# Decayed linear attention and two feed-forward layers on one core: moving the token sums of two joint blocks from GpSimd to VectorE

## The chip, the cores and the metric

The kernel runs on one core of a Trainium2 chip. The metric is the device time of one execution in microseconds; of several executions the median is given. The trace is that of one profiled execution.

## The reference

`x` has 1536 tokens of 512 features, made by a blocked linear attention with a decay for each head; two feed-forward layers follow.

```python
x = attention(q, k, v, lam)                # (B*S, H*D) = (1536, 512)
h = x @ w_in;   g = h * tanh(softplus(h));      x = g @ w_out     # 512 -> 2048 -> 512, "mish"
h = x @ w_in2;  g = h * clip(h + 3, 0, 6) / 6;  out = g @ w_out2  # 512 -> 2048 -> 512, "hswish"
```

## The kernel before

The 1536 tokens are three blocks of 512 (`k` = 0, 1, 2). Every value that a matmul reads is a pair of fp32r numbers, a rounded high part and a low part, so a product is three matmuls. `split` makes such a pair: ScalarE writes the high part (L101), VectorE subtracts it from the source for the low part (L105).

The first layer is a loop of 48 steps (`STEPS`). Its last 16 steps finish blocks 0 and 1, whose results lie in `part[0]` and `part[1]`, each 128 x 4 x 512. The last product of block 1 is still outstanding when the loop ends: `emit_g2(STEPS - 2 + j, [f])` runs it inside the next stage, and `evacuate` (L418) adds its four pieces from PSUM to `part[1]` at the points (j, f) of `LEFT`: (1, 2), (1, 3), (2, 0), (2, 1).

The second layer is done by Strassen-like products of seven terms. The third block (k = 2) goes first, over eight weight pairs, j = 0 to 7 ("pairs" below). In each pair there are four fills, f = 0 to 3 (names a, b, c, d). A fill (L827) multiplies seven terms in all into PSUM bank 0 (in pairs 0 and 1 banks 0 and 1 in turn), ScalarE copies the bank out (L968), and VectorE adds the copies into four features (L971, L975, L978, L980). Then `gate` applies the activation (ScalarE L854, VectorE L855), `feature_sums` forms four differences on VectorE (L875, tile `FS`), and `feature_part` splits the features into the tiles `G` (in the trace `lowB` or `up`), one pair later. `second` (L846) multiplies `G` by the output weights, two pairs later (`LAG`), in four pieces between the fills (`GAPS`). So in pair j TensorE does the fills of pair j and the second products of pair j - 2, which need the second feature part of pair j - 2, made in pair j - 1. The products of `second` accumulate in PSUM banks that the outstanding product of block 1 occupied: term 6 needs the bank of the first `evacuate`, term 7 that of the second, 5 and 3 those of the others.

After the pairs, blocks 0 and 1 are multiplied jointly (`joint`, L1032), eight weight pairs again, on seven token terms `XJ[0]` to `XJ[6]`, read in the order 0, 2, 5, 4, 3, 6, 1. They are made from `part[0]` (halves B11, B21) and `part[1]` (B12, B22) by the generator `joint_sums`, which the pair loop advances at the points of `SUMS`. Four of the seven are differences; GpSimd forms them in place, on 128 x 1024 fp32 values each (L473).

Within this stage the instructions of TensorE, VectorE and ScalarE are held in program order on each engine (`hold`); those of GpSimd are not held, and run when their inputs are there. Weights come by DMA from the SyncE queue: `bring(j)` at the end of pair j fetches those of later pairs into slots (`SLOT`).

Of the kernel before, what the change touches and what calls it, by code (L numbers as in the profile page):

```python
# [16 lines left out]
ALU = mybir.AluOpType  # L17
# [5 lines left out]
def decay_attention__mish_ffn__hswish_ffn_kernel(  # L23
# [8 lines left out]
    nc = tc.nc  # L32
# [9 lines left out]
    def hold(engine, ins):  # L42
        if engine in held:
            tc.keep_in_program_order(ins)
        return ins
# [57 lines left out]
    def split_lo(lo, hi, src, scale=1.0):  # L103
        if scale == 1.0:
            hold("vector", nc.vector.tensor_tensor(out=lo, in0=src, in1=f32(hi), op=ALU.subtract))  # L105
        else:
            hold("vector", nc.vector.scalar_tensor_tensor(  # L107
                out=lo, in0=src, scalar=scale, in1=f32(hi), op0=ALU.mult, op1=ALU.subtract
            ))
# [233 lines left out]
    def split(hi, lo, src, scale=1.0, on_vector=False):  # L343
        if on_vector:
            hold("vector", nc.vector.tensor_scalar(out=hi, in0=src, scalar1=scale, scalar2=None, op0=ALU.mult))
        else:
            split_hi(hi, src, scale)
        split_lo(lo, hi, src, scale)
# [56 lines left out]
    def g_lo(n):  # L405
        split_lo(g_t[n][:, 1], g_t[n][:, 0], f_t.pop(n))
# [60 lines left out]

    def joint_sums(a, b):

        B11, B12, B21, B22 = a[:, 0:2], b[:, 0:2], a[:, 2:4], b[:, 2:4]  # L470

        def sub(o, x, y):
            nc.gpsimd.tensor_tensor(out=o, in0=x, in1=y, op=ALU.subtract)  # L473

        def put(i, src):
            split(XJ[i][:, 0], XJ[i][:, 1], src)

        put(0, B11)
        yield
        put(2, B21)  # L480
        yield
        sub(B11, B12, B11)
        sub(B12, B22, B12)
        put(1, B22)
        sub(B22, B22, B11)
        sub(B21, B21, B22)
        yield
        put(3, B11)
        yield
        put(4, B12)  # L490
        yield
        put(5, B22)
        yield
        put(6, B21)
        yield

    def words(flat, i):
# [77 lines left out]
    def operand(slot, i):  # L575
        at = 512 * i
        for ap in SLOT[slot]:
            if at < ap.shape[1]:
                return ap[:, at:at + 512].rearrange("p (a n) -> p a n", a=2)
            at -= ap.shape[1]  # L580
# [226 lines left out]
    def acc_of(j):  # L807
        return ACC if j < NPAIR else ACCS[(j - SECONDS) // NPAIR]

    def block_of(j):  # L810
        return NBLK - 1 if j < NPAIR else (j - SECONDS) // NPAIR

    def pair_of(j):
        if j < NPAIR:
            return down[j]
        j -= SECONDS
        return j if j < NPAIR else 2 * NPAIR - 1 - j
# [14 lines left out]
    def whole(*ms):  # L832
        return tuple((m, (0, 1)) for m in ms)

    def second(j, parts):
        at = j + LAG if j < NPAIR else j
        nth = j % NPAIR if j < NPAIR else (j - SECONDS) % NPAIR
        first, last = nth == 0, nth == NPAIR - 1
        slot = slot_at[at][pair_of(j), 1]
        for m, halves in parts:  # L840
            gi, wi = SECOND[m]
            g = G[j][0][:, gi] if gi < 3 else G[j][1][:, gi - 3]
            w, acc = operand(slot, wi), BANK[:, acc_of(j)[m]].rearrange("p (s n) -> p s n", s=2)
            for i in halves:
                for q, (a, b) in enumerate(PASS):
                    hold("tensor", nc.tensor.matmul(  # L846
                        acc[:, i], lhsT=g[:, a, i * 128:i * 128 + 128], rhs=w[:, b],
                        start=(first and i == 0 and q == 0), stop=(last and q == 2), skip_group_check=True,
                    ))
            if last and (j < LAST or m != 3):  # L850
                close(block_of(j), m, acc_of(j))
# [11 lines left out]
    def features(j):  # L863
        if j < NPAIR:
            return FH[j % 2]
        return FJ[pair_of(j)][:, 1024 * block_of(j):1024 * block_of(j) + 1024].rearrange("p (i n) -> p i n", i=4)
# [10 lines left out]
    def feature_part(j, i):  # L877
        g, src = G[j][i], (features(j)[:, 1:4], FS[j % 2])[i]
        split(g[:, :, 0], g[:, :, 1], src)
# [15 lines left out]
    def close(k, m, acc):  # L895
        def scaled(o, m):
            hold("scalar", nc.scalar.activation(out=o, in_=BANK[:, acc[m]], func=ACTF.Copy, scale=SIXTH))

        def added(o, m, b):
            hold("vector", nc.vector.scalar_tensor_tensor(  # L900
                out=o, in0=BANK[:, acc[m]], scalar=SIXTH, in1=b, op0=ALU.mult, op1=ALU.add
            ))

        if not seen:
            if k == NBLK - 1:
                tile_ = stage_p.tile([128, 4, 512], F32, tag="st2", name="rest")
                rest[:] = [tile_[:, i] for i in range(4)]
            else:
                rest[:] = [work[:, 2048:2560], work[:, 2560:3072], two[:, 0], two[:, 1]]
        p1, p7, c12, c21 = rest  # L910
        c11, c22 = p1, p7
        q = [x.rearrange("p (s n) -> p s n", s=2) for x in rest]
        seen.add(m)
        if m == 1:
            scaled(p1, 1)
        elif m == 7:
            added(p7, 7, c12)
        elif m == 4 and not {6, 7} <= seen:
            scaled(c21, 4)
        elif m == 6:  # L920
            added(c12, 6, p1)
        if m == 7 and 4 in seen:
            plus(c21, c21, p7)
            store(k, 1, 0, q[3])
        elif m == 4 and {6, 7} <= seen:
            added(c21, 4, p7)
            store(k, 1, 0, q[3])
        if m in (2, 6) and {2, 6} <= seen:
            added(c11, 2, p1)
            store(k, 0, 0, q[0])  # L930
        if m == 5:
            added(c12, 5, c12)
        if {4, 5, 6, 7} <= seen and m in (4, 5):
            added(c22, 5, p7)
            store(k, 1, 1, q[1])
        if m == 3:
            added(c12, 3, c12)
            store(k, 0, 1, q[2])
        if len(seen) == 7:
            seen.clear()  # L940
# [12 lines left out]

    GAPS = (whole(1) + ((6, (0,)),), ((6, (1,)),) + whole(7), whole(4, 2), whole(5, 3))
    LEFT = ((1, 2), (1, 3), (2, 0), (2, 1))
    SUMS = ((0, 1), (0, 3), (2, 3), (4, 1), (5, 1), (6, 1), (7, 1))
    made = joint_sums(part[0], part[1])
    held.update(("tensor", "vector", "scalar"))
    for j in range(NPAIR):
        F = FH[j % 2]  # L960
        if j == 0:
            g_lo(STEPS - 1)
        for f, (name, ms) in enumerate(FILLS):
            bank_ = BANK[:, f % 2 if j < LAG else 0]
            fill(j, ms, bank_)
            n = 256 * len(ms)
            c = COPY[name]
            hold("scalar", nc.scalar.activation(out=c, in_=bank_[:, 0:n], func=ACTF.Copy))  # L968
            c = c.rearrange("p (i n) -> p i n", n=256)
            if f == 1:  # L970
                hold("vector", nc.vector.tensor_tensor(  # L971
                    out=F[:, 2:4], in0=COPY["a"].unsqueeze(1).to_broadcast([128, 2, 256]), in1=c, op=ALU.add
                ))
            elif f == 2:
                hold("vector", nc.vector.tensor_tensor(  # L975
                    out=F[:, 0:4:3], in0=F[:, 3:4].to_broadcast([128, 2, 256]), in1=c, op=ALU.add
                ))
                hold("vector", nc.vector.tensor_tensor(out=F[:, 1], in0=F[:, 0], in1=c[:, 1], op=ALU.add))  # L978
            elif f == 3:
                hold("vector", nc.vector.tensor_tensor(out=F[:, 0:4:3], in0=F[:, 0:4:3], in1=c, op=ALU.add))  # L980
            if j < LAG:
                emit_g2(STEPS - 2 + j, [f])
            else:
                second(j - LAG, GAPS[f])
            if f == 0 and j in (1, 2):
                FS.append(g_p.tile([128, 4, 256], F32, tag="g", name=f"FS{j}"))
            if f == 0 and j > 0:
                gates(j - 1, 0, 3)
                feature_sums(j - 1)
            elif f == 3:  # L990
                gates(j, 1, 1)
            elif j > 0:
                feature_part(j - 1, f - 1)
            if (j, f) in LEFT:
                evacuate(STEPS - 1, [LEFT.index((j, f))])
            if (j, f) in SUMS:
                next(made)
        bring(j)
    assert next(made, None) is None
    gates(NPAIR - 1, 0, 3)  # L1000
    second(NPAIR - 2, whole(1, 4, 2))
    feature_sums(NPAIR - 1)
    for i in range(2):
        feature_part(NPAIR - 1, i)
    second(NPAIR - 2, whole(6, 7, 5, 3))
    bring(NPAIR)
    second(NPAIR - 1, whole(*CLOSING))
# [139 lines left out]
```

## Time and profile before

| | us |
|---|---|
| median of 3 runs | 556.02 (555.74 to 556.15) |
| the profiled execution | 555.68 |
| its span, first to last instruction | 553.4 |
| the third block's eight pairs in the span | 301 to 382 |
| the joint products | 392.6 to 468.8 |

The rows below are from the profiled execution, whose time lies 2.28 us above its span. Times of a row count from the span's start. In a timeline, a row is a start, a duration, the engine, the line, the operation, output<-inputs with their shapes, and a count; in brackets is how long the engine had been idle before it, and what ended the idle time. Rows of a count above one merge instructions that follow each other. Matmuls are pipelined, so the durations of neighbouring rows overlap. PE is TensorE, DVE VectorE, ACT ScalarE, POOL GpSimd.

### The profile page before, as it was taken

The numbers are of one execution on the slowest core, as the hardware profiler recorded it, in microseconds if no ns is written. First come the engines' busy times: TensorE is split into PE (matmuls) and PEld (weight loads), VectorE is DVE, ScalarE is ACT, GpSimd is POOL, SyncE is SP. The second block draws the span as 40 slices with busy tenths as digits, with TensorE's granted clock in tenths as the row PEclk, the third lists the DMA queues.
The fourth block names the chain that finished last, engine by engine and source line by source line (L and its number), as shares of the span: only waits on it lengthen the run. The fifth ranks groups of instructions, "written<-read, shape, count | busy, mean of one in ns | idle before, by whom it ended". The sixth has DMA issues, their size and how long they took to land.

```text
span 553.4 us, 8899 instructions
## 1 busy us (share of the span) xinstructions
PE 543.8 (98%) x3552; PEld 475.2 (86%) x3552; DVE 392.6 (71%) x590; ACT 288.8 (52%) x425; POOL 33.5 (6%) x28
## 2 busy tenths in 40 slices
PE   8999999999999999999999989999999999999997
PEld 4887888888888888888888979999888888999996
DVE  6668875561136767796772899988677889978853
ACT  2457898873255756867482644655132434433420
POOL 1761000000000000000000033000000000000000
PEclk9999999999999999999999998999999999999999
DMA  8995556450045998889979953978655467961832
GB/s 288 411 398 205 174 195 200 153 167 25 0 153 208 370 357 278 324 307 427 371 275 411 428 230 125 379 259 324 246 189 210 165 234 252 386 295 55 292 130 77
DMA packets 23625, 137.99 MB, mean 249 GB/s; under 512 B 2208, under 2 KB 5408, under 8 KB 17440
## 3 DMA queue, kind: packets, MB, share of 16 engines
q1 hardware_dynamic: 23584, 137.43, 66.0%
q8 instruction: 28, 0.46, 0.3%
q14 instruction: 13, 0.11, 0.1%
HBM read 104.91 MB, written 32.51 MB: 248 GB/s over the span
## 4 chain that ended last, share of the span: by engine, by line
PE 94%; DVE 3%; DMA 2%; issue 0%; SPq 0%; ACT 0%; DVEq 0%; ACTq 0%
PE bank L371 24%; PE bank L380 24%; PE bank L846 21%; PE bank L1032 14%; PE bank L827 7%; PE bank L194 2%; PE bank L242 2%; DMA raw<-att 2%; PE bank L248 1%; PE bank L234 1%; DVE FS L875 1%; DVE part L418 0%; DVE work L978 0%; SPq L152 0%; ACT X L101 0%
## 5 line engine op out<-in xcount | busy, mean ns | idle before, releaser
L105 DVE TENSOR_TENSOR g<-x,g 128x512 fp32r<-128x512 f32 x48 | 33.0, 690 | 55.3 <-ACT g L401 51.6
L380 PE MATMUL bank<-g,up 128*128 128x512 f32 x288 | 70.3, 389 | 0.0
L371 PE MATMUL bank<-X,up 128*128 128x512 f32 x288 | 69.2, 389 | 0.0
L400 ACT ACTIVATE x<-bank 128x512 f32<-128x512 f32 x48 | 28.5, 593 | 69.6 <-PE bank L371 69.6
L371 PEld LDWEIGHTS bank<-X,up 128*128 128x128 f32 x288 | 54.1, 188 | 11.2
L380 PEld LDWEIGHTS bank<-g,up 128*128 128x128 f32 x288 | 53.6, 188 | 10.6
L371 PE MATMUL bank<-X,lowA 128*128 128x512 f32 x180 | 43.2, 389 | 0.0
L380 PE MATMUL bank<-g,lowA 128*128 128x512 f32 x180 | 43.2, 389 | 0.0
L380 PEld LDWEIGHTS bank<-g,lowA 128*128 128x128 f32 x180 | 33.8, 188 | 7.0
L371 PEld LDWEIGHTS bank<-X,lowA 128*128 128x128 f32 x180 | 33.8, 188 | 7.0
L107 DVE SCALAR_TENSOR_TENSOR lowA<-spare,lowA 128x1792 fp32r<-128x1792 f32 x16 | 32.4, 2023 | 10.3 <-ACT lowA L101 10.3
L846 PE MATMUL bank<-up,up 128*128 128x256 f32 x270 | 36.5, 288 | 1.6 <-DVE up L105 1.6
L846 PEld LDWEIGHTS bank<-up,up 128*128 128x128 f32 x270 | 34.6, 197 | 1.8 <-DVE up L105 1.8
L101 ACT ACTIVATE lowA<-spare 128x1792 fp32r<-128x1792 f32 x16 | 27.3, 1704 | 6.7 <-DVE spare L602 6.1
L1032 PE MATMUL bank<-X,lowA 128*128 128x512 f32 x120 | 29.3, 389 | 0.0
L401 ACT ACTIVATE g<-bank 128x512 fp32r<-128x512 f32 x48 | 28.5, 594 | 0.0
L332 ACT ACTIVATE tops<-ring 128x512 f16<-128x512 bf16 (+1 forms) x32 | 25.3, 790 | 4.0 <-DMA ring<-w 3.8
L1032 PEld LDWEIGHTS bank<-X,lowA 128*128 128x128 f32 x120 | 22.5, 188 | 4.6
L380 PE MATMUL bank<-g,lowB 128*128 128x512 f32 x108 | 25.9, 389 | 0.0
L371 PE MATMUL bank<-X,lowB 128*128 128x512 f32 x108 | 25.7, 390 | 0.0
L332 ACT ACTIVATE ring<-tops 128x512 int32<-128x512 int16 (+1 forms) x32 | 25.1, 783 | 0.8
L337 DVE SCALAR_TENSOR_TENSOR ring<-ring 128x512 int32<-128x512 int32 x24 | 16.6, 691 | 11.9 <-ACT ring L332 11.9
(192 smaller groups left out, 1038.1 us busy)
## 6 DMA issues: line engine op xcount, KB each, us to landing
wc<-lowA SPq DMA_DIRECT2D x16, 1792.0 KB, 9.9
lowA<-wc SPq DMA_DIRECT2D x15, 1792.0 KB, 9.2
up<-wc SPq DMA_DIRECT2D x13, 1792.0 KB, 8.5
ring<-w SPq DMA_DIRECT2D x24, 511.8 KB, 3.6
raw<-att SPq DMA_DIRECT2D x16, 512.0 KB, 10.2
ring<-w SPq DMA_DIRECT2D x8, 1023.5 KB, 7.2
spare<-w SPq DMA_DIRECT2D x8, 1023.5 KB, 8.1
early<-att SPq DMA_DIRECT2D x8, 512.0 KB, 10.3
```

The lines of the kernel that those rows point to most:

```text
L101: hold("scalar", nc.scalar.activation(out=hi, in_=src, func=ACTF.Copy, scale=scale))
L105: hold("vector", nc.vector.tensor_tensor(out=lo, in0=src, in1=f32(hi), op=ALU.subtract))
L107: hold("vector", nc.vector.scalar_tensor_tensor(out=lo, in0=src, scalar=scale, in1=f32(hi), op0=ALU.mult, op1=ALU.subtract))
L332: ins = nc.scalar.activation(out=o, in_=i, func=ACTF.Copy, scale=scale)
L337: hold("vector", nc.vector.scalar_tensor_tensor(out=head if dest is None else dest.bitcast(I32), in0=rest, scalar=13, in1=head, op0=ALU.lo ...
L371: hold("tensor", nc.tensor.matmul(h, lhsT=W[t][:, a, kt * 128:kt * 128 + 128], rhs=X[k][:, b, kt, :], start=(kt, a, b) == order[0], stop=( ...
L380: hold("tensor", nc.tensor.matmul(y[e], lhsT=l, rhs=r, start=(first and i == 0), stop=(last and i == 2),))
L400: hold("scalar", nc.scalar.activation(out=x, in_=h, func=ACTF.Mish))
L401: hold("scalar", nc.scalar.activation(out=g[:, 0], in_=h, func=ACTF.Mish))
L827: hold("tensor", nc.tensor.matmul(bank_[:, 256 * i:256 * i + 256], lhsT=w[:, a, kt * 128:kt * 128 + 128], rhs=x[:, b, kt], start=(i == 0 a ...
L846: hold("tensor", nc.tensor.matmul(acc[:, i], lhsT=g[:, a, i * 128:i * 128 + 128], rhs=w[:, b], start=(first and i == 0 and q == 0), stop=( ...
L1032: hold("tensor", nc.tensor.matmul(h, lhsT=w[:, a, kt * 128:kt * 128 + 128], rhs=XJ[xi][:, c, kt], start=(kt == 0 and q == 0), stop=(kt == ...
```

## The change

The four differences are formed by VectorE, held in program order, and in another order and with other intermediates: T1 = B12 - B11, T2 = B22 - T1, T3 = T2 - B11, T4 = B21 - T2. T1 and T2 lie where B12 lay, T3 where B11 lay, T4 where B21 lay.

- At the start of pair 0, before its first fill: the splits of B11 and B21 (terms 0 and 2), and T1. T1 is taken there from the unfinished `part[1]`; the two pieces that `evacuate` adds later at (1, 2) and (1, 3) complete it.
- At (3, 1): the split of T1 (term 3). At (4, 1): T2. At (4, 3): T3. At (5, 1): the split of T2 (term 5). At (5, 3): T4. At (6, 1): the split of T3 (term 4). At (7, 1): the split of T4 (term 6).
- After pair 7 and its last feature parts: the split of B22 (term 1).

Before, the splits of terms 0 and 2 stood at (0, 1) and (0, 3), all four differences and the split of term 1 at (2, 3), and those of terms 3, 4, 5, 6 at (4, 1), (5, 1), (6, 1), (7, 1).

```diff
--- before.py
+++ after.py
@@ -467,31 +467,34 @@
 
     def joint_sums(a, b):
 
-        B11, B12, B21, B22 = a[:, 0:2], b[:, 0:2], a[:, 2:4], b[:, 2:4]
+        B11, T1, B21, B22 = a[:, 0:2], b[:, 0:2], a[:, 2:4], b[:, 2:4]
+        T2, T3, T4 = T1, B11, B21
 
         def sub(o, x, y):
-            nc.gpsimd.tensor_tensor(out=o, in0=x, in1=y, op=ALU.subtract)
+            hold("vector", nc.vector.tensor_tensor(out=o, in0=x, in1=y, op=ALU.subtract))
 
         def put(i, src):
             split(XJ[i][:, 0], XJ[i][:, 1], src)
 
         put(0, B11)
-        yield
         put(2, B21)
-        yield
-        sub(B11, B12, B11)
-        sub(B12, B22, B12)
+        sub(T1, T1, B11)
+        yield
+        put(3, T1)
+        yield
+        sub(T2, B22, T1)
+        yield
+        sub(T3, T2, B11)
+        yield
+        put(5, T2)
+        yield
+        sub(T4, B21, T2)
+        yield
+        put(4, T3)
+        yield
+        put(6, T4)
+        yield
         put(1, B22)
-        sub(B22, B22, B11)
-        sub(B21, B21, B22)
-        yield
-        put(3, B11)
-        yield
-        put(4, B12)
-        yield
-        put(5, B22)
-        yield
-        put(6, B21)
         yield
 
     def words(flat, i):
@@ -953,13 +956,14 @@
 
     GAPS = (whole(1) + ((6, (0,)),), ((6, (1,)),) + whole(7), whole(4, 2), whole(5, 3))
     LEFT = ((1, 2), (1, 3), (2, 0), (2, 1))
-    SUMS = ((0, 1), (0, 3), (2, 3), (4, 1), (5, 1), (6, 1), (7, 1))
+    SUMS = ((3, 1), (4, 1), (4, 3), (5, 1), (5, 3), (6, 1), (7, 1))
     made = joint_sums(part[0], part[1])
     held.update(("tensor", "vector", "scalar"))
     for j in range(NPAIR):
         F = FH[j % 2]
         if j == 0:
             g_lo(STEPS - 1)
+            next(made)
         for f, (name, ms) in enumerate(FILLS):
             bank_ = BANK[:, f % 2 if j < LAG else 0]
             fill(j, ms, bank_)
@@ -996,12 +1000,13 @@
             if (j, f) in SUMS:
                 next(made)
         bring(j)
-    assert next(made, None) is None
     gates(NPAIR - 1, 0, 3)
     second(NPAIR - 2, whole(1, 4, 2))
     feature_sums(NPAIR - 1)
     for i in range(2):
         feature_part(NPAIR - 1, i)
+    for _ in made:
+        pass
     second(NPAIR - 2, whole(6, 7, 5, 3))
     bring(NPAIR)
     second(NPAIR - 1, whole(*CLOSING))
```

## Rows read from the trace of the kernel before

**Rows 1.** The page, part 1: busy time of TensorE, share of the span.

```profile
PE 543.8 (98%) x3552; PEld 475.2 (86%) x3552; DVE 392.6 (71%) x590; ACT 288.8 (52%) x425; POOL 33.5 (6%) x28
```

**Rows 2.** Waits of TensorE from 296 to 400 us: total, times, longest.

```profile
PE bank L846 <- DVE up L105: 1.6, 1, 1.6
PE bank L846 <- DVE part L418: 0.5, 1, 0.5
PE bank L827 <- ACT work L968: 0.4, 1, 0.4
```

**Rows 3.** TensorE timeline: first fill of pairs 2 to 5; end of pair 7.

```profile
316.49 0.87 PE L827 MATMUL bank<-X,up 128*128 128x256 f32 x6
...
327.68 0.88 PE L827 MATMUL bank<-X,lowB 128*128 128x256 f32 x6
...
341.80 0.88 PE L827 MATMUL bank<-X,lowA 128*128 128x256 f32 x6
...
352.12 0.88 PE L827 MATMUL bank<-X,up 128*128 128x256 f32 x6
...
382.34 5.20 PE L846 MATMUL bank<-lowA,lowB 128*128 128x256 f32 x42
```

**Rows 4.** Stretches: busy us by engine, granted TensorE clock, DMA share, GB/s.

```profile
317.00:332.00 15.00, 12.32 (x98) 11.54 (x96) 14.82 (x19) 6.73 (x12) 5.46 (x2) 1.00 0.62 244
333.00:335.00 2.00, 2.00 (x12) 2.00 (x11) 1.97 (x3) 0.80 (x2) 1.44 (x1) 0.50 0.45 190
335.00:337.00 2.00, 2.00 (x13) 2.00 (x13) 2.00 (x2) 0.53 (x1) 1.92 (x2) 0.67 0.00 0
352.28:362.36 10.08, 10.08 (x86) 10.08 (x86) 8.76 (x15) 5.84 (x9) 0.00 (x0) 1.00 0.94 371
```

**Rows 5.** VectorE timeline, third block, to 372 us.

```profile
299.51 0.69 DVE L105 TENSOR_TENSOR g<-x,g 128x512 fp32r<-128x512 f32 x1 [4.75 <-ACT g L401]
304.58 0.69 DVE L971 TENSOR_TENSOR work<-work 128x512 f32<-128x512 f32 x1 [4.38 <-ACT work L968]
...
312.23 0.76 DVE L875 TENSOR_TENSOR FS<-work 128x256 f32<-128x256 f32 x2
...
315.89 0.43 DVE L978 TENSOR_TENSOR work<-work,two 128x256 f32<-128x256 f32 x1
...
317.37 0.68 DVE L418 TENSOR_TENSOR part<-part,bank 128x512 f32<-128x512 f32 x1
...
320.56 2.78 DVE L875 TENSOR_TENSOR FS<-work 128x256 f32<-128x256 f32 x2
...
327.44 2.50 DVE L978 TENSOR_TENSOR work<-work,two 128x256 f32<-128x256 f32 x1
329.87 1.21 DVE L105 TENSOR_TENSOR up<-FS,up 128x1024 fp32r<-128x1024 f32 x1
...
334.06 5.04 DVE L875 TENSOR_TENSOR FS<-work 128x256 f32<-128x256 f32 x2
...
350.73 1.22 DVE L105 TENSOR_TENSOR up<-FS,up 128x1024 fp32r<-128x1024 f32 x1
...
354.03 0.69 DVE L855 SCALAR_TENSOR_TENSOR work<-x,work 128x512 f32<-128x512 f32 x1 [0.88 <-ACT x L854]
```

**Rows 6.** GpSimd timeline, third block: start, duration, line, operation.

```profile
319.99 2.73 POOL L473 TENSOR_TENSOR part<-part,part 128x1024 f32<-128x1024 f32 x1 [276.51 <-DVE part L418]
326.94 2.73 POOL L473 TENSOR_TENSOR part<-part 128x1024 f32<-128x1024 f32 x1 [4.21 <-DVE part L418]
333.56 5.25 POOL L473 TENSOR_TENSOR part<-part,part 128x1024 f32<-128x1024 f32 x2 [3.90 <-DVE X L105]
```

**Rows 7.** ScalarE timeline, start of the third block.

```profile
301.82 0.38 ACT L968 ACTIVATE work<-bank 128x256 f32<-128x256 f32 x1 [2.35 <-PE bank L827]
...
304.44 1.05 ACT L101 ACTIVATE X<-part 128x1024 fp32r<-128x1024 f32 x1
```

**Rows 8.** VectorE timeline after pair 7.

```profile
389.09 4.70 DVE L900 SCALAR_TENSOR_TENSOR rest<-bank,rest 128x512 f32<-128x512 f32 x7 [1.21 <-PE bank L846]
```

More of the change, by code (lines that the diff above doesn't have):

```diff
@@ L478, in joint_sums @@
         put(0, B11)
+        put(2, B21)
+        sub(T1, T1, B11)
         yield
-        put(2, B21)
+        put(3, T1)
         yield
-        sub(B11, B12, B11)
-        sub(B12, B22, B12)
-        put(1, B22)
-        sub(B22, B22, B11)
-        sub(B21, B21, B22)
-        yield
-        put(3, B11)
-        yield
-        put(4, B12)
-        yield
-        put(5, B22)
-        yield
-        put(6, B21)
+        sub(T2, B22, T1)
[10 more added lines that the diff above has]
+        yield
+        put(1, B22)
         yield
```

## The prediction

> **What bounds the kernel now.** I read the page's busy times first: TensorE is busy for 98% of the span [rows 1], so only time in which it waits, or runs at a lower clock, can be won. Next come the waits of TensorE in the stretch that the change touches [rows 2]. There are three, 1.6, 0.5 and 0.4 us, together 2.5 us; two are for VectorE and one is for a ScalarE copy.
>
> To see what they cost in all, I take the pairs' lengths from the first fill of each [rows 3]. Pairs 5 to 7 take (382.34 - 352.12) / 3 = 10.07 us each. Pair 2 takes 327.68 - 316.49 = 11.19, pair 3 takes 14.12 and pair 4 takes 10.32. Pairs 2 to 7 have the same number of matmuls, so the surplus is 1.12 + 4.05 + 0.25 = 5.42 us. That is more than the 2.5 us of waits. Part of the rest is the clock: from 333 to 335 us the granted clock is 0.50 of full, the lower of the two levels (1.2 GHz), and over 335 to 337 it averages 0.67 [rows 4]. In these 4 us TensorE loses 2 x 0.50 + 2 x 0.33 = 1.66 us; before that it had just waited. The remaining 1.2 us are shorter hold-ups: about 0.4 in pair 2 and 0.25 in pair 4, where a product stands for VectorE without a row of its own in the waits, and the matmuls that straddle a wait.
>
> Why is VectorE late? From 317 to 332 us it is busy for 14.82 of 15.00 us [rows 4], but not with more work. Its rows show two sums of 128 x 256 that take 0.76 us in pair 1 and 2.78 in pair 2, one of 128 x 256 that takes 0.43 and then 2.50, and again two sums of 5.04 for 0.76 [rows 5]. The stretching is 2.02 + 2.07 + 4.28 = 8.37 us. GpSimd's differences start at 319.99, 326.94 and 333.56 and end at 322.72, 329.67 and 338.81 [rows 6]; the stretched VectorE rows end at 323.34, 329.94 and 339.10, that is 0.62, 0.27 and 0.29 us after GpSimd. Each starts while GpSimd runs and is freed when it ends. The second stretched instruction ends at 329.94; the low part behind it runs from 329.87 to 331.08 [rows 5], and for just this low part TensorE waits its 1.6 us [rows 2]. The third stretch covers the time of the lowered clock; I count no further loss for it but the 0.25 of pair 4.
>
> **The change, part by part.**
>
> *Removed:* four differences on GpSimd, 2.73 + 2.73 + 5.25 = 10.7 us of its time [rows 6], and with them the 8.37 us of stretching. GpSimd has no other work in this stage, so nothing is left to stretch.
>
> *Added:* four differences of 128 x 1024 on VectorE. The nearest row, a subtraction of the same shape from SBUF to SBUF, takes 1.21 to 1.22 us [rows 5], so 4 x 1.22 = 4.9 us. The net for VectorE is 4.9 - 8.4 = -3.5 us. What matters is where they lie.
>
> *Start of pair 0.* ScalarE gets two high parts of 1.05 us [rows 7], 2.10 in all. It was idle for 2.35 us before its copy at 301.82, so from 299.47 it is done at 301.57: hidden. VectorE ends its low part of the last step at 300.20 and has nothing until 304.58, 4.38 us of idle [rows 5]. The first new low part must wait for its high part, 299.47 + 1.05 = 300.52; two low parts and T1 make 300.52 + 3 x 1.22 = 304.18, still 0.40 before the next row. Cost 0. If the cover were gone by a few tenths, the copy of fill a would be late by as much, and its bank is not filled again before fill c. T1 waits for no piece of the outstanding product, because it reads the unfinished `part[1]`.
>
> *Pairs 0 to 2.* Two splits leave (0, 1) and (0, 3), and the four differences with a split leave (2, 3). The split at (0, 3) stood in VectorE's queue ahead of pair 1's work, which ran without a gap up to `evacuate` at 317.37 to 318.05 [rows 5]. Term 6 of pair 2 needs that bank after one fill and one term, 316.49 + 0.72 + 0.72 = 317.93 (six matmuls of 0.12 us each, 42 + 42 of them make the 10.07 us). So 318.05 was too late by 0.1 and more with the restart; up to 1.2 us less in the queue puts it in time. I take the whole of pair 2's surplus as gone; the other end is that 0.4 us of it stays.
>
> *Pair 3.* The split of T1 stands at (3, 1). The pair's load becomes that of pair 5, where VectorE with one such split is busy for 8.76 of 10.08 us [rows 4]. Cost 0.
>
> *Pairs 4 and 5.* T2 at (4, 1) takes the place of a split whose low part has the same length; ScalarE has 1.05 less. T3 at (4, 3) and T4 at (5, 3) come on top: 8.76 + 1.22 = 9.98 of 10.08 us. Both lie behind the last `gate` of their pair, right where VectorE idles for 0.88 us before the first `gate` of the next [rows 5]. So some 0.34 us of 1.22 goes on to the feature parts behind. The second feature part of pair 4 ended at 351.95 [rows 5] and is needed by term 6 of pair 5 at 352.12 + 1.44 = 353.56: 1.6 us of slack. Cost 0 for TensorE; from the other side, the three wholly in its way cost 3 x 1.22 = 3.7 us.
>
> *Here a rule stands against the change.* The Trainium skill (Perfetto Trace Analysis, Optimizing Scalar/DVE Operations) says that with VectorE saturated it may make sense to give work to ScalarE or even to GpSimd; it adds that between VectorE and GpSimd this might not help, as they share an SBUF read port. By its first half the 14.82 of 15.00 us would mean that four differences more cost their 4.9 us. By the rows 2.02 + 2.07 us of those 14.82 are stretching, VectorE was filled by the helper itself, and the differences cost nothing.
>
> *After pair 7.* The split of term 1 comes behind the last feature part. VectorE idles for 1.21 us there before it closes the outputs [rows 8]; the low part's 1.22 us fit, and term 1 is the last that the joint products read. Cost 0.
>
> *DMA.* Fetches are released by TensorE's reads, so they move with it; pairs 5 to 7 keep 10.07 us at a DMA share of 0.94 in the first of them [rows 4], and pairs 2 to 4 would only come to that pace.
>
> *Sum:* 555.68 (the profiled execution) - 5.42 = 550.3 us, a span of 548.0. The median of the three runs lies 0.34 above the profiled one, so I say 550.4. Behind 382.34 everything only moves forward.
>
> **The rivals.**
>
> *Some of the surplus stays (0.15).* VectorE is still full in pairs 1 and 2: the feature sums and parts of two pairs and four `evacuate` pieces meet there. If pair 2 keeps its whole 1.12 us, the time is 551.5; if a wait of half a microsecond is left in pair 3 too, about 552. For it speaks that `evacuate` was late before GpSimd had run at all (317.37 against a start at 319.99); against it, that a split leaves the queue ahead of it.
>
> *Slower: VectorE becomes the bound in pairs 4 and 5 (0.04).* At 9.98 of 10.08 us the order on one queue can make the second feature part late. It decides from 1.6 us of delay: then TensorE waits, the clock falls as in pair 3, and each of the two pairs costs what pair 3 did, 2 x 4.05, while the old surplus goes: 550.3 + 8.1 = 558.4. Against it: only 0.34 us are left over behind the idle time.
>
> *The change does not do what it says (0.04).* If the stretching is not GpSimd's doing but goes with, say, the weight fetches, it stays with VectorE, and the time is that of before, 555.5 to 556.5. Against it: three ends within 0.62 us of GpSimd's ends, and no other stretched row.
>
> **How the numbers follow.** My forecast has 0.77 and gives 549.9 to 550.9 (the 0.4 us that pair 2 may keep, and the runs' own scatter of 0.2). The range reaches to the first rival's upper end: 549.8 to 552.2. Measurement can tell about 0.2%, 1.1 us. Faster by more: 0.77 + 0.15 = 0.92; within: 0.04; slower: 0.04.
>
> **What would show it.** Right: no GpSimd row after 50 us; no VectorE sum of 128 x 256 over 0.5 us; four new subtractions of 1.22 us, the first before 304.6; all pairs from 2 on near 10.07 us; no lowered clock at 333; the pairs end near 377. Wrong: a TensorE wait for a feature part in pair 5 or 6, or for `evacuate` in pair 2, or sums that are stretched with GpSimd idle.

## The result, and the profile after

The changed kernel takes 550.41 us (median of 5 runs, 549.72 to 550.49), against 556.02 for the kernel before (5 runs). The ratio is 0.9896, 95% interval 0.9882 to 0.9911. Its profiled execution took 550.01 us, with a span of 548.2.

First the page's busy times of the kernel after. TensorE is at 99% of the span, and GpSimd has 10.6 us less to do, which is what its differences took [rows 1]; in this section and below, [rows n] are the rows of the kernel before.

```profile
PE 540.4 (99%) x3552; PEld 473.3 (86%) x3552; DVE 389.4 (71%) x594; ACT 288.6 (53%) x425; POOL 22.9 (4%) x24
```

The list of TensorE's waits from 296 to 400 us, which had three entries before [rows 2], is empty. Its timeline shows the first fill of pairs 2 to 5 and the end of pair 7; the lines of the source have moved by three (L827 is L830, L846 is L849), those of the loop over pairs by four (L971 is L975).

```profile
316.60 0.87 PE L830 MATMUL bank<-X,up 128*128 128x256 f32 x6
...
326.67 0.88 PE L830 MATMUL bank<-X,lowB 128*128 128x256 f32 x6
...
336.75 0.88 PE L830 MATMUL bank<-X,lowA 128*128 128x256 f32 x6
...
346.83 0.88 PE L830 MATMUL bank<-X,up 128*128 128x256 f32 x6
...
377.07 5.20 PE L849 MATMUL bank<-lowA,lowB 128*128 128x256 f32 x42
```

Pair 2 takes 326.67 - 316.60 = 10.07 us, pairs 3 and 4 take 10.08 each, and pairs 5 to 7 take (377.07 - 346.83) / 3 = 10.08. Before, it was 11.19, 14.12, 10.32 and 10.07 [rows 3]. The six pairs together went from 65.85 to 60.47 us, 5.38 less. The span fell by 5.2: pair 0 starts 0.11 later than before, and the part behind the pairs is 0.07 longer (548.2 - 377.07 against 553.4 - 382.34).

The stretches, in the columns of [rows 4]: length, busy us of the engines, granted clock, DMA share and GB/s.

```profile
317.00:332.00 15.00, 15.00 (x127) 15.00 (x127) 13.81 (x25) 8.03 (x14) 0.00 (x0) 1.00 0.72 283
333.00:335.00 2.00, 2.00 (x19) 2.00 (x18) 1.97 (x4) 1.24 (x2) 0.00 (x0) 1.00 0.04 14
335.00:337.00 2.00, 2.00 (x19) 2.00 (x19) 1.71 (x3) 1.12 (x2) 0.00 (x0) 1.00 0.03 8
346.83:356.91 10.08, 10.08 (x86) 10.08 (x85) 9.60 (x15) 5.85 (x9) 0.00 (x0) 1.00 0.96 376
```

The clock is at full from 333 to 337 us, where it had been at 0.50 and 0.67. Pair 5 has VectorE busy for 9.60 of 10.08 us, with a split and a difference in it.

VectorE's timeline, with the rows that answer to [rows 5] and [rows 8]:

```profile
300.57 2.36 DVE L105 TENSOR_TENSOR X<-part,X 128x1024 fp32r<-128x1024 f32 x2 [0.25 <-ACT X L101]
302.85 1.22 DVE L474 TENSOR_TENSOR part<-part,part 128x1024 f32<-128x1024 f32 x1
304.69 0.69 DVE L975 TENSOR_TENSOR work<-work 128x512 f32<-128x512 f32 x1 [0.63 <-ACT work L972]
...
316.87 0.68 DVE L418 TENSOR_TENSOR part<-part,bank 128x512 f32<-128x512 f32 x1
...
320.06 0.76 DVE L878 TENSOR_TENSOR FS<-work 128x256 f32<-128x256 f32 x2
...
324.92 0.43 DVE L982 TENSOR_TENSOR work<-work,two 128x256 f32<-128x256 f32 x1
...
347.49 1.22 DVE L474 TENSOR_TENSOR part<-part,part 128x1024 f32<-128x1024 f32 x1
348.75 0.69 DVE L858 SCALAR_TENSOR_TENSOR work<-x,work 128x512 f32<-128x512 f32 x1
...
354.85 1.22 DVE L105 TENSOR_TENSOR lowB<-FS,lowB 128x1024 fp32r<-128x1024 f32 x1
...
382.52 1.22 DVE L105 TENSOR_TENSOR X<-part,X 128x1024 fp32r<-128x1024 f32 x1
383.82 4.70 DVE L903 SCALAR_TENSOR_TENSOR rest<-bank,rest 128x512 f32<-128x512 f32 x7
```

The reader should see four things. The two low parts and T1 end at 304.07, before the next row at 304.69. The two feature sums at 320.06 and the addition at 324.92 have their short times, 0.76 and 0.43, which had been 2.78 and 2.50. The first evacuation starts 0.27 us after the start of pair 2 (316.87), where it had been 0.88 us after it (317.37 against 316.49). T3 at 347.49 fills the idle time ahead of the next gate, which follows it without a gap.

### The profile page after: what moved, and what is told of

It reads as the page before. It is cut to its first block, busy times and chain, and to the rows that moved or that the text cites. A ratio compares the mean times of both kernels' runs of the same rounds, so it can differ in the third digit from the quotient of the medians.

```text
span 548.2 us, 8893 instructions
## 1 busy us (share of the span) xinstructions
PE 540.4 (99%) x3552; PEld 473.3 (86%) x3552; DVE 389.4 (71%) x594; ACT 288.6 (53%) x425; POOL 22.9 (4%) x24
## 4 chain that ended last, share of the span: by engine, by line
PE 96%; DMA 2%; DVE 0%; SPq 0%; issue 0%; ACT 0%; DVEq 0%
PE bank L371 24%; PE bank L380 24%; PE bank L849 22%; PE bank L1037 14%; PE bank L830 7%; PE bank L194 2%; PE bank L242 2%; DMA raw<-att 2%; PE bank L248 1%; PE bank L234 1%; SPq L152 0%; DVE early L216 0%; DVE X L105 0%; ACT X L101 0%; DVE two L947 0%
## 5 line engine op out<-in xcount | busy, mean ns | idle before, releaser
L380 PEld LDWEIGHTS bank<-g,up 128*128 128x128 f32 x288 | 53.6, 188 | 10.6
L849 PE MATMUL bank<-up,up 128*128 128x256 f32 x270 | 35.3, 283 | 0.0
L849 PEld LDWEIGHTS bank<-up,up 128*128 128x128 f32 x270 | 33.7, 192 | 0.0
```

Of the source, the lines that this page charges most:

```text
L380: hold("tensor", nc.tensor.matmul(y[e], lhsT=l, rhs=r, start=(first and i == 0), stop=(last and i == 2),))
L849: hold("tensor", nc.tensor.matmul(acc[:, i], lhsT=g[:, a, i * 128:i * 128 + 128], rhs=w[:, b], start=(first and i == 0 and q == 0), stop=( ...
```

## The experiments

All are built from one of the two kernels. The lengths of pairs are differences between first fills, as above; a pair without a loss is 10.07 to 10.08 us. The loss is the sum over pairs 2 to 7. Each ratio is to executions of the kernel before that were made with the run; their medians are 556.02 to 556.30 us.

| run | median us | ratio to before, 95% interval | pair 2 | pair 3 | pair 4 | later pairs | loss |
|---|---|---|---|---|---|---|---|
| before | 556.02 | | 11.19 | 14.12 | 10.32 | 10.07 | 5.4 |
| after | 550.41 | 0.9896 (0.9882, 0.9911) | 10.07 | 10.08 | 10.08 | 10.08 | 0 |
| e1, after, differences on GpSimd | 553.92 | 0.9959 (0.9946, 0.9973) | 10.07 | 10.08 | 13.30 | 10.08 | 3.2 |
| e2, before, differences on VectorE | 553.52 | 0.9950 (0.9937, 0.9962) | 10.43 | 12.32 | 10.08 | 10.08 | 2.6 |
| e3, before without differences | 551.05 | 0.9903 (0.9890, 0.9917) | 10.43 | 10.08 | 10.08 | 10.08 | 0.35 |
| e8, after, splits at old places | 550.71 | 0.9901 (0.9888, 0.9915) | 10.43 | 10.08 | 10.08 | 10.08 | 0.35 |
| e9, after, one split at its old place | 549.99 | 0.9893 (0.9878, 0.9908) | 10.43 | 10.08 | 10.08 | 10.08 | 0.35 |
| e10, before, splits first | 554.83 | 0.9978 (0.9968, 0.9988) | 10.59 | 14.12 | 10.30 | 10.07 | 4.8 |
| e4, after, two GpSimd subtractions more | 553.90 | 0.9959 (0.9943, 0.9975) | 12.81 | 11.57 | 10.08 | 10.08 | 4.2 |
| e5, after, two GpSimd memsets more | 550.53 | 0.9901 (0.9881, 0.9920) | 10.07 | 10.08 | 10.08 | 10.08 | 0 |
| e6, after, one more on VectorE | 550.23 | 0.9889 (0.9869, 0.9908) | 10.07 | 10.08 | 10.08 | 10.08 | 0 |
| e6, three more on VectorE | 555.07 | 0.9982 (0.9969, 0.9995) | 10.06 | 10.08 | 10.08 | 11.47, 12.99, 10.08 | 4.3 |

Losses of a few tenths are read from the pairs, not from the medians: pair 0 starts between 299.87 and 301.65 us in these runs, whatever the edit.

### Engine or place?

**e1: the places of after, on GpSimd.**

```diff
-            hold("vector", nc.vector.tensor_tensor(out=o, in0=x, in1=y, op=ALU.subtract))
+            nc.gpsimd.tensor_tensor(out=o, in0=x, in1=y, op=ALU.subtract)
```

> The changed kernel's places and order, but the four differences on GpSimd again. Theory (a GpSimd difference stretches VectorE's sums and low parts): T1 runs early, where VectorE idles, and costs nothing; T2, T3 and T4 follow each other from about 333 us, stretch VectorE rows by some 6 us in all, and TensorE waits in pair 3 or 4: 553 to 556 us. Rival (what helped is the new places and order of the splits and differences, on whichever engine): 550.4 us.

It took 553.92 us. TensorE's waits, GpSimd's differences, and the VectorE rows that met them:

```profile
PE bank L849 <- DVE lowB L105: 1.6, 1, 1.6
PE bank L830 <- ACT work L972: 1.1, 1, 1.1
```

```profile
268.68 2.42 POOL L474 TENSOR_TENSOR part<-part,part 128x1024 f32<-128x1024 f32 x1 [224.98 <-DVE part L418]
333.90 2.78 POOL L474 TENSOR_TENSOR part<-part 128x1024 f32<-128x1024 f32 x1 [62.80 <-DVE X L105]
336.76 5.80 POOL L474 TENSOR_TENSOR part<-part,part 128x1024 f32<-128x1024 f32 x2
```

```profile
334.46 2.51 DVE L982 TENSOR_TENSOR work<-work,two 128x256 f32<-128x256 f32 x1
336.89 3.41 DVE L105 TENSOR_TENSOR lowB<-FS,lowB 128x1024 fp32r<-128x1024 f32 x1
340.22 2.88 DVE L984 TENSOR_TENSOR work<-work,two 128x512 f32<-128x512 f32 x1
```

T1 ran at 268.68, even earlier than its place, as nothing holds GpSimd in order. T2 starts at 333.90, and T3 and T4 follow at once until 342.56. In that time VectorE gets through three instructions, which take 2.51, 3.41 and 2.88 us instead of 0.42, 1.22 and 0.69: 6.5 us of stretching, for three differences that cost 3.7 us on VectorE. TensorE waits for the second feature part and then for a copy, and pair 4 loses 3.2 us. So new order and places, as far as GpSimd takes them up, keep 2.2 of the 5.4 us, and the rival as I had put it, 550.4 us on whichever engine, falls. But T1, T3 and T4 did not run at their new places, which only VectorE is held to. A run with GpSimd held to them was not made. By an estimate it might cost little: a stretch is 2.0 to 2.2 us, and VectorE took two differences, 2.3 us, in each of two pairs without a loss (e6 below). Whether VectorE is needed once the differences are spread is therefore not shown.

**e2: the places of before, on VectorE.** The same line, the other way, in the kernel before.

> The kernel before with its own places and order, but the four differences on VectorE. Theory: no stretched row is left; the four differences and a split in one burst of 5 x 1.2 us at (2, 3) make VectorE late once, TensorE waits some 2 us in pair 3, with a lower clock behind it perhaps 4: 552.5 to 554.5 us. Rival of the places: 555.5 to 556.5 us.

It took 553.52 us. TensorE's wait, and VectorE's burst behind pair 2:

```profile
PE bank L827 <- ACT two L968: 2.0, 1, 2.0
```

```profile
328.30 1.22 DVE L473 TENSOR_TENSOR part<-part,part 128x1024 f32<-128x1024 f32 x1
329.55 1.23 DVE L473 TENSOR_TENSOR part<-part 128x1024 f32<-128x1024 f32 x1
330.69 1.22 DVE L105 TENSOR_TENSOR X<-part,X 128x1024 fp32r<-128x1024 f32 x1
331.94 2.48 DVE L473 TENSOR_TENSOR part<-part,part 128x1024 f32<-128x1024 f32 x2
334.34 0.69 DVE L855 SCALAR_TENSOR_TENSOR work<-x,work 128x512 f32<-128x512 f32 x1
```

No row is stretched, but the four differences and a split stand in a row from 328.30 to 334.42, ahead of the first gate of pair 3, which had been ready. A ScalarE copy stands behind a high part that waits for this gate; it is late, TensorE waits 2.0 us, and pair 3 loses 2.2. The engine alone thus keeps 2.8 of the 5.4 us. In this execution the clock stays at full behind the wait; columns as above:

```profile
336.00:338.00 2.00, 1.56 (x13) 1.56 (x14) 1.97 (x4) 1.45 (x2) 0.00 (x0) 1.00 0.00 0
338.00:340.00 2.00, 2.00 (x19) 2.00 (x18) 1.97 (x4) 1.23 (x2) 0.00 (x0) 1.00 0.03 8
```

**e3: the differences left out.**

```diff
         def sub(o, x, y):
-            nc.gpsimd.tensor_tensor(out=o, in0=x, in1=y, op=ALU.subtract)
+            pass
```

> The kernel before without the four differences (left out: terms 3 to 6 are then undifferenced halves); nothing runs on GpSimd or in its place on VectorE. Theory: no stretched row, no wait but the first evacuation in pair 2, which is 0.1 to 0.4 us late: 550.3 to 550.9 us. Rival (the stretching belongs to the weight fetches): 555.5 us.

It took 551.05 us, and pair 2 of 10.43 us is its only loss. Taking GpSimd's work away gives back 5.07 of the 5.42 us, with the same weight fetches. The theory that the fetches stretch VectorE falls.

### What of GpSimd's work stretches VectorE?

**e4: two subtractions more on GpSimd in the changed kernel; e5: two memsets.** Both write into a place that a later split overwrites.

```diff
             if (j, f) in SUMS:
                 next(made)
+            if (j, f) == (2, 3):
+                for _ in range(2):
+                    nc.gpsimd.tensor_tensor(out=XJ[5][:, 0], in0=part[0][:, 0:2], in1=part[0][:, 2:4], op=ALU.subtract)
```

In e5 the last line is `nc.gpsimd.memset(f32(XJ[5][:, 0]), 0.0)`.

> The changed kernel with two subtractions of 128 x 1024 more on GpSimd at (2, 3), into a place that is overwritten later. Nothing else waits for them. Theory: they run from about 326 to 331 us and VectorE's rows with two inputs from SBUF stretch until they end, 4 to 5 us; fill d of pair 3 waits about 2 us, with the clock 2 to 4: 552.4 to 554.5 us. Rival (no stretching by GpSimd; VectorE waited for inputs): 550.4 us.

> The same with two memsets of 128 x 1024 on GpSimd in place of the subtractions: GpSimd writes as much and reads nothing. If any GpSimd instruction stretches VectorE, the rows that meet the memsets are as long as these; if only one that reads SBUF does, no VectorE row is stretched: 550.4 us. I expect the second.

e4 took 553.90 us. GpSimd, VectorE, and the stretches with the granted clock:

```profile
320.77 5.20 POOL L1004 TENSOR_TENSOR up<-part 128x1024 fp32r<-128x1024 f32 x2 [278.34 <-PE bank L830]
```

```profile
320.97 2.76 DVE L975 TENSOR_TENSOR work<-work 128x512 f32<-128x512 f32 x1
323.66 3.13 DVE L105 TENSOR_TENSOR up<-work,up 128x768 fp32r<-128x768 f32 x1
326.71 0.67 DVE L418 TENSOR_TENSOR part<-part,bank 128x512 f32<-128x512 f32 x1
```

```profile
326.00:328.00 2.00, 0.56 (x4) 0.57 (x5) 1.98 (x3) 0.00 (x0) 0.00 (x0) 1.00 0.00 0
328.00:330.00 2.00, 2.00 (x14) 2.00 (x13) 1.98 (x3) 0.99 (x2) 0.00 (x0) 0.62 0.53 100
330.00:332.00 2.00, 2.00 (x11) 2.00 (x11) 1.87 (x5) 0.66 (x2) 0.00 (x0) 0.53 0.80 308
```

The subtractions ran at 320.77, some 5 us ahead of where I had put them, because the part of the slot that they write was read for the last time by a fill in the middle of pair 2. Their effect is the expected one at another place: an addition of 0.69 takes 2.76 us, a low part of 0.95 takes 3.13, the fourth evacuation comes at 326.71, 11.3 us after the start of its pair (315.44) instead of 7.0, and TensorE waits 2.5 us for it. Then the granted clock is 0.62 and 0.53 over 4 us, that is the lower level (0.50) for most of them. The loss is 2.73 us in pair 2 and 1.49 in pair 3.

e5 took 550.53 us.

```profile
322.48 1.97 POOL L1004 MEMSET up<- 128x1024 f32 x2 [278.27 <-PE bank L830]
```

```profile
322.76 0.69 DVE L975 TENSOR_TENSOR work<-work 128x512 f32<-128x512 f32 x1
323.36 0.95 DVE L105 TENSOR_TENSOR up<-work,up 128x768 fp32r<-128x768 f32 x1
```

The memsets run from 322.48 to 324.45; the same addition and the same low part fall into that time and take 0.69 and 0.95 us. No pair loses anything. So GpSimd's writing alone does not stretch VectorE; its instructions that read from SBUF do. All of these read two inputs; no run has one with a single input.

e1 shows the other half, in VectorE's rows under T1 (268.68 to 271.10):

```profile
269.06 0.68 DVE L418 TENSOR_TENSOR part<-part,bank 128x512 f32<-128x512 f32 x1
269.66 2.53 DVE L337 SCALAR_TENSOR_TENSOR spare<-spare 128x1024 int32<-128x1024 int32 x1
```

The addition that reads one input from SBUF and one from PSUM keeps its 0.68 us. The next instruction reads both from SBUF and takes 2.53 us; in the changed kernel it takes 1.22. A stretched instruction ends its own length, less 0.13 us, behind GpSimd's: 0.29 us for a sum of 0.42 (before), 0.82 for a low part of 0.95 (e4), 1.09 for one of 1.22 (e1). These ends fit an instruction that stands until GpSimd's has ended, and not one that runs more slowly.

The Trainium skill (SBUF — State Buffer, SBUF: two separate sides) describes this: VectorE and GpSimd share a pair of SBUF ports under an exclusive lock; a VectorE instruction with two SBUF inputs contends for it only with a GpSimd instruction that reads SBUF, and the one that starts first keeps it for its whole length. The traces agree: VectorE stands for the rest of GpSimd's instruction, by the ends above, and the memsets stretch nothing. (The 0.62 us of the first stretched row before belongs to a row of two sums [rows 5, 6]; the first of them ends 0.29 us behind GpSimd's, and the second is not stretched.)

### How much can VectorE take?

**e6: one and three subtractions more at (4, 3) and at (5, 3)**, behind T3 and T4, into a place that is overwritten later.

```diff
+            if (j, f) in ((4, 3), (5, 3)):
+                for _ in range(1):
+                    hold("vector", nc.vector.tensor_tensor(out=XJ[1][:, 1], in0=part[1][:, 2:4], in1=f32(XJ[0][:, 0]), op=ALU.subtract))
```

> The changed kernel with one subtraction of 128 x 1024 more on VectorE behind T3 at (4, 3) and one behind T4 at (5, 3) (into a place that is overwritten later). Theory (1.6 us of slack in the feature parts): 1.14 us more a pair stays inside it: 550.3 to 550.6 us, no wait. Rival (VectorE is at the bound in pairs 4 and 5): 2 x 1.14 = 2.3 us, 552.7 us, more with the clock.

> The same with three subtractions at each of the two points, 3.4 us more a pair. The slack of 1.6 us is passed: TensorE waits some 1.3 us in pair 5 and some 3 us in pair 6, 4.2 in all, and a lower clock behind a wait adds up to 3.5: 554.5 to 558 us. If the time stays at 550.4, the slack was far larger than I worked out.

With one more, the time is 550.23 us and no pair loses anything; VectorE is then busy for 9.90 of the 10.00 us from 347 to 357. With three more it is 555.07 us: pair 5 loses 1.4 and pair 6 loses 2.9 us. That is close to the 1.3 and 3 that I had worked out, but by luck, since those came from the slack of a feature part. The waits of TensorE:

```profile
PE bank L830 <- ACT two L972: 3.8, 2, 2.7
```

TensorE waits for a ScalarE copy (`two`, the copy of fill c), twice, and in this execution the clock stays at full behind both waits, in all stretches of 2 us from 353 to 361 and from 365 to 371. So VectorE had more room than the nearly full share suggests, and less than 3.4 us a pair.

### Pair 2's own term

**e8: splits of terms 0 and 2 at their old places, T1 at (2, 3); e9: the split of term 2 alone at (0, 3).** The diff of e9:

```diff
         put(0, B11)
-        put(2, B21)
         sub(T1, T1, B11)
         yield
+        put(2, B21)
+        yield
...
-    SUMS = ((3, 1), (4, 1), (4, 3), (5, 1), (5, 3), (6, 1), (7, 1))
+    SUMS = ((0, 3), (3, 1), (4, 1), (4, 3), (5, 1), (5, 3), (6, 1), (7, 1))
```

> The changed kernel with the splits of terms 0 and 2 back at (0, 1) and (0, 3) and T1 at (2, 3). The prediction's step for pair 2 says that the split at (0, 3) made the first evacuation late: then pair 2 keeps 0.1 to 0.4 us of its surplus, 550.5 to 550.9 us, with the first evacuation at about 317.4. Rival (that hold-up came from GpSimd too): 550.4 us and a pair 2 of 10.07 us.

> The changed kernel with one split alone, that of term 2, back at (0, 3). Theory (this split is the one in VectorE's queue ahead of the first evacuation, since VectorE idles again behind the other): pair 2 is 10.43 us as with both splits back, all other pairs 10.08, 0.35 us lost: 550.6 to 551.0 us. Rival (the split at (0, 1) counts, or T1): pair 2 of 10.07 us, 550.4 us.

Both have a pair 2 of 10.43 us and lose nothing else. In e8 the first evacuation starts at

```profile
317.86 0.68 DVE L418 TENSOR_TENSOR part<-part,bank 128x512 f32<-128x512 f32 x1
```

which is 0.89 us behind the start of its pair 2 (316.97), as before. e9 shows that the split at (0, 3) does it by itself. The medians, 550.71 and 549.99, cannot tell 0.35 us. T1 at (2, 3) costs nothing in e8: pair 3 is 10.08. So that T1 is taken ahead of the last product is not what gained.

**e10: the kernel before with the two splits first, the differences untouched.** The two `put` calls stand in one step that runs ahead of the first fill.

> The kernel before with one part of the change alone: the splits of terms 0 and 2 at the start of pair 0; the differences stay on GpSimd and at their places. Theory: the three stretched stretches stay, about 8 us; pair 2 keeps 0.0 to 0.7 us of its 1.12 us surplus, pair 3 most of its 4.05 us: 554.6 to 556.0 us. Rival of the places: well under 554 us.

It took 554.83 us, ratio 0.9978. Pair 2 is 10.59 instead of 11.19, pairs 3 and 4 are as before. By the pairs of the profiled execution this part alone is worth 0.6 us; by the medians it is 1.2 (0.7 to 1.8, from the interval). Either way it is the small part.

## Why the prediction was right

- **The term of 5.42 us.** Predicted from the pairs' surplus; measured 5.38 between the same two points, and 550.41 for 550.4 in the median. That the medians agree to 0.01 us is luck: the executions scatter by 0.8 us. The profiled execution fell by 5.67, of which 0.47 lies outside the span (1.81 us around it, against 2.28).
- **VectorE late because of GpSimd.** Shown by e3 (no differences, no stretched row), e1 and e4 (GpSimd again, stretched again) and e5 (no SBUF reads, no stretching).
- **The waits and the clock.** The changed kernel has neither, as the sum had it: no wait in the list, and a granted clock of 1.00 in the stretches above. But the 1.66 us that the working gave to the clock are no cost of their own. The third stretch, for which it counted only the 0.25 of pair 4, would have held TensorE back for nearly as long at full clock, by these ScalarE rows of the kernel before:

```profile
339.93 1.06 ACT L101 ACTIVATE lowB<-FS 128x1024 fp32r<-128x1024 f32 x1 [1.59 <-DVE FS L875]
340.90 0.58 ACT L968 ACTIVATE two<-bank 128x512 f32<-128x512 f32 x1
```

  The high part waits for the feature sums behind the stretch, which end at 339.90. The copy of fill d, behind it, ends at 341.48 and frees the bank for the first fill of pair 4, which started at 341.80 [rows 3]. So a full clock would have saved 0.3 us at most. The executions of the kernel before agree: with the experiments there are 41, eight of them with a mean granted clock of 1.000, and these have a median of 556.26 us, against 556.09 for the twenty with 0.995 to 0.997. (Two with 0.992 took 557.7 and 557.8.) The sum came out all the same, because the 5.42 us were read from the pairs and not added up from the parts.
- **Pair 2.** The 0.4 us that I kept as the other end, for the split at (0, 3), is 0.35 in e8 and e9, and nothing in the changed kernel.
- **Start of pair 0.** Predicted end of T1 304.18, measured 304.07; the copy of fill a is not late.
- **Pairs 4 and 5.** Predicted load 9.98 of 10.08 us; measured 9.60 in pair 5, and 9.61 in pair 6, where T4 runs. Most of the 0.38 lies in the base. The 8.76 us came from the pair 5 before, which VectorE entered late: its first gate starts 0.35 us into the pair, in pairs 6 and 7 it is 0.06. Pair 7, with a split and no difference, has 8.47 us before and after. T3 adds 1.13 to that, less than its row's 1.22, because neighbouring rows overlap. Cost 0, as predicted.
- **Slack.** Here the working was less good than its result. The 1.6 us belonged to a feature part ahead of T3 in the queue; the one behind T3 ends at 354.85 + 1.22 = 356.07 and is needed at 356.91 + 1.44 = 358.35, 2.3 us of slack. And what gave way first with three more subtractions was not a feature part but the copy of fill c on ScalarE, which waits behind a high part that waits for VectorE. My price of a slower outcome, 2 x 4.05 us, took the clock along; in the profiled execution of that run it did not fall, and the ten executions took 553.39 to 556.38 us, not 558.4.
- **After pair 7.** The low part at 382.52 ends at 383.74, and the first closing row starts at 383.82, 0.73 us behind ScalarE's start of its own at 383.09, against 0.79 before. No cost.
- **The rule against it.** That a full VectorE may gain from work given to GpSimd (the Trainium skill, Perfetto Trace Analysis, Optimizing Scalar/DVE Operations) does not hold here: e1 gives it three differences in the pairs, and VectorE loses 6.5 us to save 3.7. The rule's own second half, the shared port, is what the runs show.

What the parts are worth: the engine alone 2.8 us (e2), the new order with GpSimd kept, at such places as it took, 2.2 (e1), both 5.4. VectorE removes the stretching, and spreading the differences, over pairs 0, 4 and 5, removes the burst that takes its place.

What stays open: whether spread differences would cost anything on GpSimd, if it were held to the new places; and why the clock fell behind some waits and not behind others (below). No run beats the changed kernel by more than the scatter, and none of them points to such a version: TensorE has no wait left from 296 to 400 us.

## What to carry to other kernels

When an engine is busy without a gap, compare the durations of its like instructions before calling it overloaded: here VectorE was full because two sums of 0.76 us took 2.78 and 5.04, and giving it more work made it less full. Count an offload to GpSimd with what it takes from VectorE: some 2.0 to 2.2 us for a difference that VectorE does in 1.22, wherever it meets an instruction with both inputs in SBUF. And place moved work where its queue idles: in one burst with a split the same four instructions cost 2.2 us (e2), spread they cost nothing.

## What the runs showed of the hardware

In the profiled executions the clock did not follow the length of a wait. It fell behind waits of 1.6 and 0.4 us before and behind 2.5 us in e4, and stayed at full behind 2.0 us in e2, behind 1.6 and 1.1 in e1, and behind two that make 3.8 us, the longest 2.7, in the run with three more. In the kernel before, the three waits lay within some 7 us (326 to 332), and the clock fell about 1 us after the last; in e4 one wait ended at 327.4, and the clock fell within the 2 us after 328. In e1 the two waits lay as close (340.4 and 344.3) and it did not fall.

Each of these is one execution, and executions of one kernel differ. Of the ten of e4, two have a mean granted clock of 1.000 and took 552.05 and 552.92 us; six have 0.995 or 0.996 and took 553.08 to 555.49, the profiled one among them. Of the five of e2, the profiled one and another have 0.999 and took 552.67 and 552.98; three have 0.996 or 0.997 and took 553.52 to 554.65. So one trace does not say whether a wait in a kernel brings the clock down, and the cause stays open.

Two memsets of 128 x 1024 took 1.97 us on GpSimd, two subtractions of that size 5.20.
